# State-space matmuls with two lag halves in 32 weight columns, and six more sets of attention tiles on VectorE

## The chip, the cores and the metric

The kernel runs on one core of one Trainium2 chip. The metric is the device time of one execution in microseconds. Before the change the median of three runs is 829.91 us, with 829.02 us as the lowest and 830.75 us as the highest.

## The reference

The result mixes two branches of the same input `x` (2048 rows of 512 channels, bf16):

- `a`: softmax attention without a mask, 32 heads of 16 channels, `softmax(q k^T / 4) v`, then the product with `wo`. The scores are 32 x 2048 x 2048 numbers, and each needs an exponential.
- `b`: a long convolution for each channel. The kernel `K[d, l]` of 2048 lags is the real part of a sum over 128 complex states, `sum_n C[d,n] dB[d,n] exp(l dt A[d,n])`; `b = conv(x, K) + x * Dskip`, causal.
- The gate is `g = sigmoid(sum(x * gate_w))`, one number for each row, and the output is `g * a + (1 - g) * b`.

```python
    x = A_x
    g = _sigmoid((x * gate_w).sum(-1, keepdims=True))
    a = _A_ref(x, A_wqkv, A_wo)
    b = _B_ref(x, B_A_re, B_A_im, B_B_re, B_B_im, B_C_re, B_C_im, B_log_dt, B_Dskip)
    return g * a + (1 - g) * b
```

## The kernel before

**Attention.** The scores come in 2048 tiles of 128 keys by 512 queries, three tiles to a group, so 683 groups. For each group TensorE makes the scores in one of two PSUM buffers, `SC0` and `SC1` (`qk`), ScalarE takes the exponential of the group in one instruction (`ex`, line 907) into a ring of slots `ET` and, from group `NSG` on, also `EX`, and TensorE multiplies the result with the values into `OA` (`pv`). A score buffer is free again when all three of its tiles were read.

**Sets on VectorE.** Some tiles skip ScalarE. A set takes four tiles, each as the third tile of its own group, so such a group has only two tiles (1024 columns) for ScalarE. VectorE reads each of the four from PSUM with one `tensor_scalar` (`bits`, line 928), which makes the bit pattern of a bf16 power of two, and then finishes the four together (`batch`: two masks, line 939, and one product, line 947, on 2048 columns). The table `WIN` says in which groups sets may start, how many groups lie between two of them, and, as its last number, how much idle VectorE time a set must find. The kernel before has 71 sets.

**Convolution.** The channels go in 16 blocks of 32. For each block VectorE multiplies tables (`tables`, line 1197), TensorE makes the lags by matmuls with 32 weight columns of stride 128 (`kstage`, tiles `T` and `Z`), VectorE turns them round (`Kt`, `Ks`, lines 1233 to 1239), and they go to DRAM (`kd`) and back as Toeplitz pieces `H` (line 1295). `ystage` (line 1320) convolves: for each of 128 pieces there are 16 lag steps `m`, and in each four matmuls side by side in four column groups of the array, with 16 weight columns and 128 - 8m moving columns from `U`. VectorE multiplies the sum with 1 - g (line 1327, tile `Yst`), and it goes through DRAM (`yd`) to `Yl`.

**Gate and output.** `gate` computes g by 16 matmuls over `xT` (line 1356). `outs` multiplies the attention rows with `wo` in 16 row tiles `lt`, and VectorE makes `MB * g + Yl` (line 1418); the last four tiles get their last quarter at the very end (line 1605).

**What sets the order.** There is no order at run time: a planner on the host (`Sched`, `Prog`) keeps one clock for each engine and queue, from a cost `c` written at each operation, and writes each engine's instruction list. After each exponential it fills TensorE, VectorE and the DMA queue of SyncE with pieces of the other work, by their due times. It models the loading of TensorE's instructions in blocks of 256 (`BLOCK`, `pt`), and adds matmuls on zeros (`zero`, tile `wm`) so that the array's activity stays at a wanted level; `a` at each matmul is its share of that. All matmuls are recorded through one helper, so the profile shows all of them at line 661; they are told apart by tiles.

## Time and profile before

| What | Value |
|---|---|
| median of three runs | 829.91 us |
| the profiled execution | 830.66 us, span 828.7 us |
| ScalarE busy | 808.6 us (98%) |
| VectorE busy | 743.4 us (90%) |
| TensorE matmul busy | 686.8 us (83%), 15986 instructions |
| weight loads | 311.3 us (38%) |
| mean DMA rate | 112 GB/s |

The span is the time from the first to the last instruction in the trace, and the execution is some 2 us longer. Durations of neighbouring instructions on one engine overlap by some tens of nanoseconds, so a group's mean is more than the distance at which instructions follow each other; where that matters the count in a window of known length is used. In rows of groups the columns are: line, engine, operation, output<-input, shapes and count, then busy time and mean ns of one, then the idle time before them and what ended it. In rows of windows an engine's busy time is followed by the count of its instructions.

### The profile page before, as it was taken

The page shows a single profiled execution, that of the slowest core. Times are in us where ns is not written, and L with a number is a line of the kernel's source. Part 1 is how long each engine was busy: PE and PEld are TensorE (multiplying, and loading weights), DVE is VectorE, ACT ScalarE, POOL GpSimd, SP SyncE. Part 2 cuts the span into 40 slices and gives each one's busy share as a digit, 9 for nine tenths or more (in the row PEclk, how much of TensorE's full clock was granted, in tenths as well). Part 3 has the DMA queues.
Part 4 walks back from the last instruction along what each step waited for, and adds up shares of the span by engine and source line. Part 5 has one row for each costly group of instructions (what it writes and reads, how often), then busy time and mean ns, then how long its engine had stood idle before and what let it go on. Part 6 is the DMA issues. An engine that isn't in the chain of part 4 may idle for free.

```text
span 828.7 us, 35337 instructions
## 1 busy us (share of the span) xinstructions
PE 686.8 (83%) x15986; PEld 311.3 (38%) x16013; DVE 743.4 (90%) x1231; ACT 808.6 (98%) x692; POOL 10.2 (1%) x16
## 2 busy tenths in 40 slices
PE   7778787888788888898888988888887888878885
PEld 3232332333244444444454434444442444422221
DVE  7998998999999998899889889888998979699973
ACT  7999999999999999999999999999999999999995
POOL 4000000000000000000000000000000000000000
PEclk9999999999999999999999989999999999999998
DMA  9453001243566654654565555545566655410000
GB/s 194 99 109 52 7 8 17 52 132 112 165 161 172 151 138 125 171 150 121 133 139 129 151 135 131 137 121 142 128 166 118 184 148 149 104 24 21 23 32 26
DMA packets 182111, 92.75 MB, mean 112 GB/s; under 512 B 119237, under 2 KB 176966, under 8 KB 181578
## 3 DMA queue, kind: packets, MB, share of 16 engines
q1 hardware_dynamic: 180234, 89.58, 43.9%
q8 instruction: 126, 2.06, 1.1%
q10 hardware_dynamic: 1728, 0.92, 0.6%
q14 instruction: 23, 0.19, 0.1%
HBM read 64.47 MB, written 17.32 MB: 99 GB/s over the span
## 4 chain that ended last, share of the span: by engine, by line
ACT 91%; DVE 4%; PE 3%; DMA 1%; issue 0%; ACTq 0%; DVEq 0%
ACT ET L907 71%; ACT EX L907 19%; DVE DZ L928 2%; PE SC L661 1%; PE MB L661 1%; PE OA L661 1%; DVE DU L947 1%; DMA ldt<-in_B_log_dt_dram 1%; DVE fo L1418 0%; DVE DU L939 0%; DVE OT L963 0%; DVE DZ L939 0%; ACT L907 0%; ACT L1508 0%; ACTq L623 0%
## 5 line engine op out<-in xcount | busy, mean ns | idle before, releaser
L907 ACT ACTIVATE ET<-SC 128x1536 bf16<-128x1536 f32 (+1 forms) x530 | 648.9, 1538 | 3.4 <-PE SC L661 3.3
L661 PE MATMUL SC<-Qm,KT 32*128 32x512 bf16 x2048 | 277.6, 386 | 122.8 <-ACT ET L907 85.9
L928 DVE TENSOR_SCALAR DZ<-SC 128x512 uint16<-128x512 f32 x284 | 189.7, 685 | 35.2 <-PE SC L661 33.7
L907 ACT ACTIVATE EX<-SC 128x1024 bf16<-128x1024 f32 (+1 forms) x153 | 184.3, 1370 | 2.1 <-PE SC L661 1.9
L661 PEld LDWEIGHTS SC<-Qm,KT 32*128 32x128 bf16 x2048 | 70.6, 91 | 288.1 <-ACT ET L907 200.2
L661 PE MATMUL OA<-ET,VE 128*32 128x512 bf16 x1394 | 154.2, 392 | 1.4 <-ACT ET L907 0.9
L661 PE MATMUL OA<-wm 128*32 128x256 bf16 (+3 forms) x773 | 153.9, 354 | 1.2 <-DVE wm L714 1.2
L661 PEld LDWEIGHTS MB<-U,H 128*16 128x16 bf16 x8192 | 113.3, 108 | 46.1 <-issue 29.1
L661 PE MATMUL MB<-U,H 128*16 128x72 bf16 (+15 forms) x8192 | 128.1, 198 | 2.3 <-issue 2.2
L947 DVE TENSOR_TENSOR DU<-DZ,DU 128x2048 bf16<-128x2048 bf16 x71 | 87.3, 1233 | 0.8
L979 DVE TENSOR_TENSOR T<-B,DL 128x512 bf16<-128x512 bf16 x192 | 69.6, 418 | 0.0
L661 PEld LDWEIGHTS OA<-ET,VE 128*32 128x32 bf16 x1394 | 39.2, 93 | 77.3 <-issue 72.9
L661 PE MATMUL OA<-EX,VE 128*32 128x512 bf16 x370 | 55.6, 394 | 0.1
L661 PEld LDWEIGHTS MB<-T,Z 128*32 128x32 bf16 x2048 | 51.5, 178 | 9.1 <-issue 6.6
L661 PE MATMUL MB<-T,Z 128*32 128x64 bf16 (+1 forms) x2048 | 52.3, 246 | 0.0
L939 DVE TENSOR_SCALAR DU<-DZ 128x2048 uint16<-128x2048 uint16 x71 | 49.6, 705 | 0.7
L939 DVE TENSOR_SCALAR DZ<-DZ 128x2048 uint16<-128x2048 uint16 x71 | 49.6, 700 | 0.4
L661 PEld LDWEIGHTS OA<-wm 128*32 128x32 bf16 (+2 forms) x773 | 40.2, 95 | 13.9 <-issue 12.1
L979 DVE TENSOR_TENSOR ft<-FP,L 128x1024 f32<-128x1024 f32 (+1 forms) x32 | 34.8, 1123 | 0.4
L1327 DVE TENSOR_TENSOR Yst<-MB,gt 128x512 bf16<-128x512 f32 x32 | 21.9, 685 | 8.2 <-PE MB L661 8.2
L661 PE MATMUL OA<-DU,VE 128*32 128x512 bf16 x284 | 27.9, 383 | 0.3 <-DVE DZ L939 0.3
L661 PE MATMUL OA<-DZ,VE 128*32 128x512 bf16 x284 | 27.9, 381 | 0.0
(129 smaller groups left out, 461.4 us busy)
## 6 DMA issues: line engine op xcount, KB each, us to landing
H<-gm_kd SPq DMA_DIRECT2D x256, 128.0 KB, 3.4
U<-gm_xs SPq DMA_DIRECT2D x96, 136.0 KB, 2.9
U<-gm_xs SPq DMA_DIRECT2D x32, 134.2 KB, 3.0
T<-B SPq DMA_DIRECT2D x32, 128.0 KB, 2.6
gm_bd<-B16s SPq DMA_DIRECT2D x3, 1024.0 KB, 5.6
B<-gm_bd SPq DMA_DIRECT2D x12, 256.0 KB, 4.0
gm_kd<-Ks SPq DMA_DIRECT2D x64, 40.0 KB, 2.9
gm_xs<-xP SPq DMA_DIRECT2D x16, 136.0 KB, 4.8
```

The costliest lines, as they stand in the source:

```text
L661: op("PE", lambda t: t.matmul(out(), lhsT(), rhs(), start=start, stop=stop, skip_group_check=True, **kw), R, W, c=c, lat=.15, a=a, cfg=cfg)
L907: op("ACT", lambda a: a.activation(E(at, [[1, 512 * n]]), sc(0, [[1, 512 * n]]), AF.Exp, scale=DH ** -0.5), [(sc, i, g) for i in range(n)] ...
L928: op("DVE", lambda v: v.tensor_scalar(z.u16(512 * k, [[1, 512]]), sc(1024, [[1, 512]]), XS, XB, ALU.mult, ALU.add), [(sc, 2, g)], [(z, k, ...
L939: op("DVE", lambda v: v.tensor_scalar(t.u16(0, [[1, 2048]]), z.u16(0, [[1, 2048]]), a, o, ALU.bitwise_and, ALU.bitwise_or), R, W, c=.07 + ...
L947: op("DVE", lambda v, h=h, n=n: v.tensor_tensor(u(n * h, [[1, n]]), z(n * h, [[1, n]]), u(n * h, [[1, n]]), ALU.mult), R + [(u, 0, ("m", i ...
L979: op(eng, lambda v: v.tensor_tensor(o(), a(), b_(), f), R, W, c=c)
L1327: op("DVE", lambda v, w=w, h=h: v.tensor_tensor(Yst(1024 * w + 64 * h, [[128, R8], [4, 16], [1, 4]]), MB(0, [[1, R8], [R8, 16], [NC, 4]]), ...
```

## The change

- The lag steps of `ystage` go from 16 to 8. A weight tile now has 32 columns: for each of 16 phases one column for lag steps 0 to 7 and one for 8 to 15, on neighbouring PSUM partitions. The matmuls have 128 to 72 moving columns. The second half's result belongs 1024 rows later, so `Yst` and `yd` hold both halves, `Yl` gets the first and a new tile `Yl2` the second.
- `outs` adds both halves for row tiles 8 to 15 by two matmuls with the identity `idb` into the same PSUM sum; VectorE then only copies. So that the sum is right, the attention rows of these tiles get g earlier: one more product on the reciprocals `Rz` for query blocks 16 and up, with g in the layout `gq`.
- `gate` reads `xT` in contiguous rows of 512; its result goes out in pieces of four, `gt` is loaded for both halves by eight transfers and `gq` by five more.
- The table products go from twelve of 512 columns for a block to four of 1024 and four of 512. The lags' copy into `Ks` is four instructions in place of three.
- `H` is loaded by one transfer of 256 KB in place of two of 128 KB, with four buffers in place of five; `EX` is used from group 290 on in place of 214.
- The planner: a new model of TensorE's instruction loading, the batch of a set at a higher priority, and `WIN` asks for less idle time for each set. It comes to 77 sets.

```diff
-NSG = 214
+NSG = 290
...
-WIN = ((190,400,3,5,.9),(400,560,5,5,.9),(560,668,5,5,.6))
+WIN = ((190,400,3,5,.4),(400,560,5,5,.4),(560,674,5,5,.3))
...
+TM = (2, 1)
...
-NHB = 5
+NHB = 4
...
-HN = 2
+HN = 1
...
-FETCH = 3.4
-KEEP = 24
+PHASE = 191
+LEAD = 20
+F1 = 4.5
+F2 = 5.1
+KEEP = 8
+FORE = 12
...
-        if eng == "PE":
-            self.pt += [self.tm["PE"]] * 2
...
+        if eng == "PE" and len(self.pt) + 1 >= self.edge():
+            at = max(at, self.land())
...
+        w = self._record(eng, fn, deps, eng, i, R, W)
+        if eng == "PE":
+            b = self.edge()
+            self.pt += [at] * (2 + max(w - 1, 0))
+            if len(self.pt) > b:
+                self.av.append(max(self.pt[b - LEAD] + F1, self.av[-1] + F2))
...
+    def edge(self):
+        return (len(self.av) - 1) * BLOCK + PHASE
+
+    def land(self):
+        return self.av[-1]
...
-                    k = len(self.p.pt) - BLOCK + KEEP + 2 * len(t.seg)
-                    if k >= 0 and t.up > 0:
-                        e = max(e, self.p.pt[k] + FETCH - t.cost)
+                    k = self.p.edge() - len(self.p.pt) - 2 * sum(isinstance(a, tuple) for a in t.seg)
+                    if t.up > 0:
+                        e = max(e, self.p.land() - t.cost - max(k - KEEP, 0) / FORE)
...
+    sb("Yl2", 8 * D)
+    sb("gq", 32, FP32)
...
-            sch.add(batch(i), 1)
+            sch.add(batch(i), 0)
...
+        qc = b // 8
+        if qc >= 2:
+            op("DVE", lambda v: v.tensor_tensor(Rz(16 * w, [[16, n], [4, 4], [1, 4]]), Rz(16 * w, [[16, n], [4, 4], [1, 4]]),
+                                                B["gq"](4 * (qc - 2), [[0, n], [1, 4], [8, 4]]), ALU.mult),
+               [(Rz, x) for x in K] + [(B["gq"], j) for j in range(4)], [(Rz, x) for x in K], c=.12)
...
-                for m in range(3):
-                    Dm = B[("DL16", "DL64", "DL80")[m]]
-                    for k, (xr, yr) in enumerate(((0, 0), (1, 2), (1, 0), (0, 1))):
-                        yield ("DVE", H5)
...
+                DT = B["DT"]
+                for k, (xr, yr) in enumerate(((0, 0), (1, 2), (1, 0), (0, 1))):
+                    m = 0
+                    for w in TM:
+                        yield ("DVE", dv(512 * w, 2))
+                        tt("DVE", lambda k=k, m=m, w=w, Tm=Tm: Tm((k // 2 * 112 + (16, 64)[k % 2] + 16 * m) * CB, [[16 * CB, w], [2 * CB, 8], [1, 2 * CB]]),
...
-                    ch = 32 * (blk % 4) + 16 * (j // 2) + 2 * (j % 2) + 4 * (k % 4) + k // 4
+                    ch = 32 * (blk % 4) + 4 * (j // 2) + 2 * (j % 2) + 8 * (k % 4) + k // 4
...
-            op("DVE", lambda v, q=q: v.tensor_copy(Ks(5 * HW * q + HW, [[16, 4], [HW, 4], [1, 16]]), Kt(256 * q, [[64, 4], [16, 4], [1, 16]])),
+            op("DVE", lambda v, q=q: v.tensor_copy(Ks(5 * HW * q + HW, [[8, 4], [HW // 2, 8], [1, 8]]), Kt(256 * q, [[64, 4], [8, 8], [1, 8]])),
...
-        op("DVE", lambda v: v.tensor_copy(Ks(1, [[5 * HW, 2], [16, 4], [1, 15]]), Kt(48, [[256, 2], [64, 4], [1, 15]])),
-           [(Kt, 0, blk), (Ks, "z")], [(Ks, 1, blk)], c=.17)
+        for q in range(2):
+            op("DVE", lambda v, q=q: v.tensor_copy(Ks(q * HW // 2 + 1 - q, [[5 * HW, 2], [8, 4], [1, 7 + q]]), Kt(48 + 7 * q, [[256, 2], [64, 4], [1, 7 + q]])),
+               [(Kt, 0, blk), (Ks, "z")], [(Ks, (1, q), blk)], c=.13)
...
-    UN = 16 * UW - R8 + 1
-    UL = 16 * UW // UN4
+    Yst, yd, Yl, Yl2 = B["Yst"], B["yd"], B["Yl"], B["Yl2"]
+    UN = 4 * UW - R8 + 1
+    UP = 16 * UW // UN4
...
-                n = UL if i < UN4 - 1 else UN - UL * (UN4 - 1)
-                dma("SP", lambda e, v=v, U=U, i=i, n=n: e.dma_start(U(UL * i, [[1, n]]), xs.dram(v * 16 * UW + R8 - 1 + UL * i, [[D * UW, T], [-1, R8], [1, n]])),
+                dma("SP", lambda e, v=v, U=U, i=i: e.dma_start(U(UP * i, [[1, UN]]),
+                                                               xs.dram((v // 2 * 32 + v % 2 * 4) * UW + 2 * UP * i + R8 - 1, [[D * UW, T], [-1, R8], [1, UN]])),
...
-                for m in range(NM):
+                for m in range(NM // 2):
                     n = NC - R8 * m
-                    c = max(.0305, .0005 + n / 2400)
-                    if m in (0, 3, 7, 11):
-                        yield ("PE", sum(max(.0305, .0005 + (NC - R8 * x) / 2400) for x in range(m, m + (4 if m else 3))))
+                    c = n / 2400 + .0005
+                    if m % 4 == 0:
+                        yield ("PE", sum((NC - R8 * x) / 2400 for x in range(m, m + 4)))
                     for j in range(4):
-                        mm(lambda q=q, j=j, n=n: MB(NC * q + NC - n, [[1, n]], 32 * j, T),
-                           lambda j=j, m=m, H=H: H(j * NM + m, [[HW, T]]),
+                        mm(lambda q=q, j=j, n=n: MB(NC * q + NC - n, [[1, n]], 32 * j, 32),
+                           lambda j=j, m=m, H=H: H(j * NM // 2 + m, [[HW // 2, 2 * T]]),
                            lambda q=q, j=j, n=n, U=U: U((4 * j + q) * UW + 1, [[1, n]]),
-                           [(H, i, hu) for i in range(HN)] + [(U, i, u) for i in range(UN4)], ky, q + m == 0, m == NM - 1, pos=(0, 32 * j), c=c if j == 0 else 0,
-                           a=n // 8, cfg="C")
+                           [(H, i, hu) for i in range(HN)] + [(U, i, u) for i in range(UN4)], ky, q + m == 0, m == NM // 2 - 1, pos=(0, 32 * j), c=c if j == 0 else 0,
+                           a=n // 4, cfg="C")
...
-            op("DVE", lambda v, w=w, h=h: v.tensor_tensor(Yst(1024 * w + 64 * h, [[128, R8], [4, 16], [1, 4]]), MB(0, [[1, R8], [R8, 16], [NC, 4]]),
+            op("DVE", lambda v, w=w, h=h: v.tensor_tensor(Yst(1024 * w + 4 * h, [[128, R8], [8, 16], [1, 4]]), MB(0, [[1, R8], [R8, 16], [NC, 4]]),
...
-            dma("SP", lambda e, j=j: e.dma_start(yd.dram(512 * blk + 128 * j, [[8192, T], [T * 8192, R8], [1, 128]]),
-                                                 Yst(1024 * w, [[128, R8], [1, 128]], 32 * j, T)),
-                [(Yst, (w, h), blk) for h in range(2)], [(yd, (blk, j))], c=.6, lat=3.5, b=.15)
+            dma("SP", lambda e, j=j: e.dma_start(yd.dram(512 * blk + 128 * j, [[8192, 2 * T], [8192 * 2 * T, R8], [1, 128]]),
+                                                 Yst(1024 * w, [[128, R8], [1, 128]], 32 * j, 2 * T)),
...
-        for h in range(2):
...
-            dma("SP", lambda e, h=h: e.dma_start(Yl(512 * blk + 256 * h, [[64, 4], [1, 64]]), yd.dram(512 * blk + 64 * h, [[8192, P], [128, 4], [1, 64]])),
-                [(yd, (blk, j)) for j in range(4)], [(Yl, (blk, h))], c=.6, lat=3, b=.42, pace=True)
+            n = 128 >> k
+            dma("SP", lambda e, k=k, y=y, n=n: e.dma_start(y(4 * n * blk, [[n, 4], [1, n]]), yd.dram(512 * blk + 8192 * k, [[8192 * 2, P], [128, 4], [1, n]])),
+                [(yd, (blk, j)) for j in range(4)], [(y, blk)], c=.6, lat=3, b=.5, pace=True)
...
-                   lambda c=c, q4=q4: xT(q4 * S + 32 * c, [[1, 32], [P, 16]]),
+                   lambda c=c, q4=q4: xT(q4 * S + 512 * c, [[1, 512]]),
...
-        op("DVE", lambda v: v.tensor_copy(gl(0, [[1, 512]]), MB(0, [[1, 512]])), [(MB, 0, 'gate')], key("gl"), c=.62)
+        op("DVE", lambda v: v.tensor_copy(gl(0, [[4, P], [1, 4]]), MB(0, [[1, P], [P, 4]])), [(MB, 0, 'gate')], key("gl"), c=.62)
...
-            dma("SP", lambda e, j=j: e.dma_start(B["gt"](0, [[16, R8], [1, 16]], 32 * j, T), B["gd"].dram(0, [[16, T], [16 * T, R8], [1, 16]])),
+            dma("SP", lambda e, j=j: e.dma_start(alt("gt", [[16, R8], [1, 16]], 32 * j), B["gd"].dram(0, [[16, T], [16 * T, R8], [1, 16]])),
...
+            yield ("SP", .6)
+            dma("SP", lambda e, j=j: e.dma_start(alt("gt", [[16, R8], [1, 8]], 32 * j + 1), B["gd"].dram(8, [[16, T], [16 * T, R8], [1, 8]])),
+                [(B["gd"], 0)], [(B["gt"], 4 + j)], c=.6, lat=2.5)
...
+        yield ("SP", .6)
+        dma("SP", lambda e: e.dma_start(B["gg"].dram(0, [[16, P], [1, 16]]), g(0, [[1, 16]])), key("g"), [(B["gg"], 0)], c=.6, lat=2.5)
+        for j in range(4):
+            yield ("SP", .6)
+            dma("SP", lambda e, j=j: e.dma_start(B["gq"](0, [[8, 4], [1, 8]], 32 * j, 32), B["gg"].dram(8, [[16, 32], [512, 4], [1, 8]])),
+                [(B["gg"], 0)], [(B["gq"], j)], c=.6, lat=2.5)
+        sch.mark("gq")
...
+            if lt >= 8:
+                for y, at, W in ((Yl, 8 * lt, 128), (Yl2, 8 * (lt - 8), 64)):
+                    yield ("PE", MM)
+                    mm(lambda: MB(0, [[1, 512]]), lambda: idb(0, [[1, P]]), lambda y=y, at=at, W=W: y(at, [[W, D // 8], [1, 8]]),
+                       [(idb, 0)] + [(y, k) for k in range(NBLK)], [(MB, 0, ('o', lt))], False, y is Yl2)
...
-            op("DVE", lambda v, lt=lt, o=o, off=off: v.scalar_tensor_tensor(o(off, [[1, D]]), MB(0, [[1, D]]), B["g"](lt, [[1, 1]]),
-                                                                            Yl(4 * lt, [[64, D // 4], [1, 4]]), ALU.mult, ALU.add),
...
+            if lt < 8:
...
+            else:
+                op("DVE", lambda v, o=o, off=off: v.tensor_copy(o(off, [[1, D]]), MB(0, [[1, D]])), [(MB, 0, ('o', lt))], W, c=.62)
...
-        op("DVE", lambda v, lt=lt, b=b, off=off: v.scalar_tensor_tensor(fo((lt % 4) * D, [[1, D]]), b(off, [[1, D]]), B["g"](lt, [[1, 1]]),
-                                                                     fp((lt - 12) * D, [[1, D]]), ALU.mult, ALU.add),
...
+        op("DVE", lambda v, lt=lt, b=b, off=off: v.tensor_tensor(fo((lt % 4) * D, [[1, D]]), b(off, [[1, D]]), fp((lt - 12) * D, [[1, D]]), ALU.add),
```

More of the change, by code (lines that the diff above doesn't have):

```diff
@@ L131, in __init__ @@
         self.pt = []
+        self.av = [0.0]
         self.marg = {}
@@ L223, in _record @@
             b.st[sl] = [{stream: idx}, {}]
+        return len(waits)
     def op(self, eng, fn, R=(), W=(), c=.1, lat=.085, a=0, cfg=None):
@@ L516, in declare @@
         sb(n, 2 * D, FP32)
-    for n in ("L16", "L64", "L80"):
-        sb("D" + n, 6 * D)
+    sb("DT", 3 * 6 * D)
     for n in ("L32", "M8", "M9"):
@@ L545, in declare @@
     B["MB"] = Buf("MB", "ps", 512, FP32)
-    for n, free in (("kd", 8 * NBLK * HR * HW), ("xs", T * D * UW), ("yd", D * S), ("bd", 8 * P * 4096), ("qd", D * S), ("od", D * S)):
+    for n, free in (("kd", 8 * NBLK * HR * HW), ("xs", T * D * UW), ("yd", 2 * D * S), ("bd", 8 * P * 4096), ("qd", D * S), ("od", D * S)):
         B[n] = Buf(n, "dr", free, BF16)
         B[n].t = nc.dram_tensor("gm_" + n, [free // P, P], BF16)
-    for n in ("gd", "gld"):
+    for n in ("gd", "gg", "gld"):
         B[n] = Buf(n, "dr", P * 16, FP32)
@@ L1024, in short @@
         yield ("DVE", .33 * w * parts)
-        op("DVE", lambda v: v.tensor_copy(d(0, [[w, parts * D], o]), x(0, [[1, parts * D], i])), [(x, 0)], [(d, 0)], c=.07 + .28 * w * parts)
+        op("DVE", lambda v: v.tensor_copy(d(at, [[w, parts * D], o]), x(0, [[1, parts * D], i])), [(x, 0)], [(d, (ky, 0))], c=.07 + .28 * w * parts)
         if neg:
@@ L1245, in kstage @@
                                                  Ks(0, [[HW, 10], [1, HW]], 32 * h, 32)),
-                [(Ks, (0, 0), blk), (Ks, (0, 1), blk), (Ks, 1, blk), (Ks, "z")], [(kd, (blk, h))], c=.7, lat=3.5, b=.26)
+                [(Ks, (a, q), blk) for a in range(2) for q in range(2)] + [(Ks, "z")], [(kd, (blk, h))], c=.7, lat=3.5, b=.26)
         sch.mark(f"kd{blk}")
@@ L1369, in gate @@
         yield ("DVE", .4)
-        op("DVE", lambda v: v.memset(B["gt"](0, [[1, NC]]), 0.0), [], [(B["gt"], j) for j in range(4)], c=.2)
+        op("DVE", lambda v: v.memset(B["gt"](0, [[1, NC]]), 0.0), [], [(B["gt"], j) for j in range(8)], c=.2)
         op("DVE", lambda v: v.tensor_scalar(gp(0, [[1, 16]]), ge(0, [[1, 16]]), 1.0, None, ALU.add), key("ge"), key("gp"), c=.17)
@@ L1388, in out_mm @@
         mm(lambda: b(off, [[1, 512]]), lambda: OnX(pi * 512 + 128 * r, [[1, 128]]), lambda: Wo(pi * D, [[1, D]]),
-           [(OnX, pi // 2 if qc < SPILL else pi), (Wo, 0)], [(b, sl, ('o', lt))], pi == first, pi == (2 if lt >= 12 and first == 0 else 3))
+           [(OnX, pi // 2 if qc < SPILL else pi), (Wo, 0)], [(b, sl, ('o', lt))], pi == first, pi == 3 and (lt < 8 or first == 3))
     def out_dma(lt):
```

37 lines of the change are left out of this document (22 added, 15 removed).

## The prediction

> **What bounds the kernel now.** I read first the page's busy shares, the chain that ended last and the groups.
>
> ```profile
> span 828.7 us, 35337 instructions
> ...
> PE 686.8 (83%) x15986; PEld 311.3 (38%) x16013; DVE 743.4 (90%) x1231; ACT 808.6 (98%) x692; POOL 10.2 (1%) x16
> ...
> ACT 91%; DVE 4%; PE 3%; DMA 1%; issue 0%; ACTq 0%; DVEq 0%
> ...
> L907 ACT ACTIVATE ET<-SC 128x1536 bf16<-128x1536 f32 (+1 forms) x530 | 648.9, 1538 | 3.4 <-PE SC L661 3.3
> ...
> L928 DVE TENSOR_SCALAR DZ<-SC 128x512 uint16<-128x512 f32 x284 | 189.7, 685 | 35.2 <-PE SC L661 33.7
> L907 ACT ACTIVATE EX<-SC 128x1024 bf16<-128x1024 f32 (+1 forms) x153 | 184.3, 1370 | 2.1 <-PE SC L661 1.9
> ```
>
> ScalarE is the bound: 98% busy, 91% of the chain, 5.5 us idle before its 683 exponentials. 284 groups have their third tile on VectorE, and one is short because 2048 is no multiple of 3: 285 exponentials of two tiles, 398 of three. Their cost comes from the chain in order of time (start, length, what) and from a stretch almost without waits (498.32 to 740 us).
>
> ```profile
> 11.59 1.45 ACT ET L907
> ...
> 13.56 53.73 ACT ET L907 x40
> ...
> 818.44 0.93 ACTq L623
> ```
>
> ```profile
> L907 ACT ACTIVATE ET<-SC 128x1536 bf16<-128x1536 f32 x63 | 94.4, 1643 | 0.0
> L907 ACT ACTIVATE ET<-SC 128x1024 bf16<-128x1024 f32 x88 | 91.1, 1237 | 0.1
> L907 ACT ACTIVATE EX<-SC 128x1024 bf16<-128x1024 f32 x42 | 45.0, 1247 | 0.0
> L907 ACT ACTIVATE EX<-SC 128x1536 bf16<-128x1536 f32 x28 | 43.8, 1632 | 0.0
> ```
>
> Three tiles take 53.73/40 = 1.343 us. The stretch holds 91 of these and 130 of two tiles in 241.7 us, so two tiles take (241.7 - 91 x 1.343)/130 = 0.919 us. A tile moved off ScalarE is worth 0.424 us. The stream from 11.59 to 818.44 us is 806.9 us; 398 x 1.343 + 285 x 0.919 = 796.4 us of it is exponentials, and 10.4 us is lost. The windows show where:
>
> ```profile
> 230.00:810.00 580.00, 496.80 (x13624) 238.51 (x13633) 523.14 (x855) 576.19 (x517) 0.00 (x0) 0.99 0.49 124
> ...
> 440.00:450.00 10.00, 9.28 (x278) 5.66 (x282) 9.96 (x17) 10.00 (x10) 0.00 (x0) 1.00 0.46 131
> ...
> 465.00:470.00 5.00, 4.72 (x109) 2.56 (x109) 4.06 (x6) 5.00 (x5) 0.00 (x0) 0.70 0.36 96
> ...
> 490.00:500.00 10.00, 9.47 (x220) 3.81 (x206) 8.35 (x14) 8.71 (x9) 0.00 (x0) 0.66 0.52 141
> ...
> 744.00:781.00 37.00, 31.75 (x275) 9.22 (x276) 36.57 (x56) 35.51 (x35) 0.00 (x0) 1.00 0.09 26
> ```
>
> Columns are PE, PEld, DVE, ACT, POOL, granted clock, DMA share, GB/s. Around 465 to 500 us the clock falls to 0.66-0.70, matmuls fill the time and ScalarE waits; at 744 to 781 us VectorE is full (36.57 of 37) and ScalarE lacks 1.5 us. From 230 to 810 us VectorE has 580.0 - 523.1 = 56.9 us free.
>
> **The change part by part.**
>
> *Six more sets on ScalarE.* 24 tiles less: 24 x 0.424 = **-10.2 us**, on the chain. One exponential more or less at the stretch's edges moves the two-tile price by 0.01 us, so the ends are -9.9 and -10.4.
>
> *The gate.* Its 16 matmuls read `xT` with a stride. They are in front of the scores on TensorE's list:
>
> ```profile
> 67.66 3.60 PE L661 MATMUL MB<-xT,gwT 128*32 128x512 bf16 x16
> ...
> 71.63 4.14 ACT L907 ACTIVATE ET<-SC 128x1536 bf16<-128x1536 f32 x3 [1.66 <-PE SC L661]
> ...
> L661 PE MATMUL MB<-xT,Wk 128*128 128x512 bf16 x52 | 16.0, 383 | 1.1 <-issue 0.9
> ```
>
> Contiguous rows of the same width cost 16.0/52 = 0.31 us each; four groups of four side by side are then some 1.2 us and not 3.6. ScalarE's wait of 1.66 us needs more than 1.9 us of delay, so it goes: **-1.7 us** (between 0 and -1.7). Its nine further transfers on SyncE's queue, and its result in pieces of four, lie between the gate and the first use of `gt`:
>
> ```profile
> L1378 SPq DMA_DIRECT2D gt<-gm_gd x4: 334/426/775, 85.1 to 87.1; - x4
> ...
> L661 PE MATMUL MB<-U,H x8192: 168/197/307, 224.0 to 727.7; 128*16 128x128 bf16 x13, 128*16 128x48 bf16 x13, 128*16 128x96 bf16 x13, 128*16 128x16 bf16 x13
> ```
>
> From 87 to 224 us there is room for a chain many times as long; without that cover the convolution would begin later by what the pieces take.
>
> *VectorE.* Work added and saved, by these rows; the first three are chain pieces from a full stretch, where distances show:
>
> ```profile
> 761.35 0.60 DVE DZ L928
> 761.95 0.60 DVE DZ L939
> ...
> 769.27 1.13 DVE DU L947
> ```
>
> ```profile
> L947 DVE TENSOR_TENSOR DU<-DZ,DU 128x2048 bf16<-128x2048 bf16 x71 | 87.3, 1233 | 0.8
> L979 DVE TENSOR_TENSOR T<-B,DL 128x512 bf16<-128x512 bf16 x192 | 69.6, 418 | 0.0
> L939 DVE TENSOR_SCALAR DZ<-DZ 128x2048 uint16<-128x2048 uint16 x71 | 49.6, 700 | 0.4
> ...
> L979 DVE TENSOR_TENSOR ft<-Z,DM 128x1024 bf16<-128x1024 bf16 x32 | 20.7, 686 | 0.4
> ...
> L969 DVE RECIPROCAL Rz<-OT 128x32 f32<-128x32 f32 x15 | 5.2, 347 | 0.0
> ...
> L1239 DVE CAST Ks<-Kt 128x120 bf16<-128x120 f32 x16 | 3.5, 218 | 0.0
> ```
>
> A set is 4 x 0.60 + 2 x 0.60 + 1.13 = 4.73 us (by mean durations 5.37), six are +28.4 (to 32.2). Table products: 192 at 69.6/192 = 0.36 become 64 at 0.36 and 64 at 20.7/32 = 0.65: -4.8; should the extra dimension of the 1024-column form cost its speed, it could not be more than two of 512 each, so 0. `Ks`: 16 more at 0.22, +3.5. The g product on `Rz`: nine at up to 0.35, +1.5 to +3. The output copies are simpler than what they replace, under 0.5. Sum **+29 us of VectorE**, 26 to 38. All of it lies beside ScalarE if it fits: of 56.9 us free some 10 go with the shorter span, so 56.9 - 10.2 - 29 = 18 us of 570 remain, 3%. What is late when it does not fit is the third tile's read: the score buffer stays taken, `qk` of the next group but one waits, then ScalarE.
>
> *TensorE.* 8192 convolution matmuls become 4096.
>
> ```profile
> L661 PEld LDWEIGHTS MB<-U,H 128*16 128x16 bf16 x8192 | 113.3, 108 | 46.1 <-issue 29.1
> L661 PE MATMUL MB<-U,H 128*16 128x72 bf16 (+15 forms) x8192 | 128.1, 198 | 2.3 <-issue 2.2
> ...
> L661 PEld LDWEIGHTS MB<-T,Z 128*32 128x32 bf16 x2048 | 51.5, 178 | 9.1 <-issue 6.6
> L661 PE MATMUL MB<-T,Z 128*32 128x64 bf16 (+1 forms) x2048 | 52.3, 246 | 0.0
> ...
> L661 PE MATMUL MB<-Wo,OnR 128*128 128x512 bf16 x40 | 13.7, 386 | 0.2 <-issue 0.2
> ```
>
> Now 128.1/8192 = 15.6 ns each, so 4096 at that price are 64 us; the nearest matmuls with 32 strided weight columns (`T,Z`) take 52.3/2048 = 25.5 ns, so 105 us. I take the latter, like in width and stride: -23 us, ends -64 and 0 (twice the price of now). Two identity matmuls for eight row tiles add 16 x 13.7/40 = 5.5 us. So TensorE has some 17 us more room, worth nothing on the chain but where TensorE is full (465 to 500 us).
>
> The Trainium skill, "TensorE: Matmul & The Clock Gate", section "LDWEIGHTS (loading the stationary operand)", has a load cost its columns divided by 1.2 in ns: 13.3 for 16 columns, 26.7 for 32. The rows agree, 113.3/8192 = 13.8 and 51.5/2048 = 25.1. By that rule 4096 loads of 32 columns take 109 us, as long as now, and the room on TensorE is nearer to 4 us than to 23; the sum below stays.
>
> *Transfers.* `H` doubles in size and is fetched by half as many transfers, with one buffer less.
>
> ```profile
> H<-gm_kd SPq DMA_DIRECT2D x256, 128.0 KB, 3.4
> ...
> B<-gm_bd SPq DMA_DIRECT2D x12, 256.0 KB, 4.0
> ```
>
> A piece lasts about (727.7 - 224.0)/128 = 3.9 us, so three pieces ahead are 11.7 us against 4.0 to land: hidden; without cover TensorE's list stands with the scores behind it. `yd` doubles and `Yl2` comes new, at a DMA share of 0.49: hidden. SyncE's queue has 128 issues less for `H` and some 9 more for the gate. `EX` from group 290: ScalarE's idle time above ends with score matmuls (3.3 and 1.9 us), never with a slot that comes free, so nothing, at worst waits like those of the last window above.
>
> *The tail.* One more product stands between reciprocal and normalization of the last block: **+0.2 us** (0 to 0.35).
>
> **The sum.** 828.7 - 10.2 - 1.7 + 0.2 = 817.0 us of span, if the other 8.7 us of loss stay: less at the clock's low place, more where VectorE is full. The profiled execution lies 1.96 us over its span and 0.75 over the median of the runs: 829.91 - 11.7 = **818.2 us**.
>
> **The rivals.**
>
> *VectorE becomes the bound (slower).* The extra 29 us leave 3% free, and reads of third tiles queue behind products of 1.13 us. Price: in the full window ScalarE lost 1.5 of 37 us, 4%; over 570 us that is 23 us, less 1.5 lost already, 818.2 + 21.5 = 839.7 us. It decides from a loss of 11.7/570 = 2.1%. For it: that window. Against: 440 to 450 us, VectorE 9.96 of 10 full and ScalarE 10.00. Chance 0.14; with 0.03 for a loss that just eats the gain.
>
> *TensorE's stretch goes.* With 4096 matmuls fewer the place at 465 to 500 us is gone and the clock holds, so half of the 8.7 us comes back: under 814 us. In that place the chain has
>
> ```profile
> 487.57 0.80 issue
> ```
>
> where TensorE waits for nothing that the profile shows; half as many convolution instructions would shorten it if it is their supply. The Trainium skill, "Runtime: NRT & Kernel Launch", section "Instruction fetch mechanics", holds the fetch to be hidden; no run here shows what this piece is. Chance 0.13.
>
> *The clock falls more often.* The new plan has other matmuls and zeros; one or two more places like 465 to 500 us, 3 us each, give 822 to 828 us. Chance 0.07.
>
> *The sets do not come.* Whether 77 sets stand in the program is fixed when it is built; they can only come and not pay, which is the first rival.
>
> **How the numbers follow.** Forecast, ScalarE the bound with about the losses of now (814 to 822 us): 0.63. With 0.13 and 0.07 faster is 0.83; same, within 0.2% or 1.7 us (about what a measurement of this kernel can tell from no change), 0.03; slower 0.14. Range 811 to 829 us: its low end is the sum with seven of the 8.7 us gone, its high end a loss on VectorE that leaves a gain of 1 us; left out are some 0.17.
>
> **What would show it.** Right: 308 reads by VectorE, two-tile exponentials 309, ScalarE still near 98% with idle under 8 us, VectorE near 94-95%, gate matmuls near 1 us with no wait behind, `U,H` matmuls between 64 and 105 us. Wrong: long waits of ScalarE for score matmuls that themselves wait for `DZ`; TensorE waiting for `H`; windows with the clock under 0.8 in number.

## The result and the profile after

The changed kernel takes 879.12 us (median of 4 runs, 876.42 to 880.24), the kernel before 829.51 us (4 runs, 829.02 to 830.75). The ratio is 1.0591, with a 95% interval from 1.0564 to 1.0618. The forecast of 818.2 us was wrong in its sign. The profiled execution took 879.35 us.

The page of the changed kernel; in rows of groups the columns are busy time, mean ns of one, idle time before and what ended it. ScalarE's records overlap by more than the tens of nanoseconds named above: in the prediction's rows of three tiles their mean is 1643 ns and their distance 1343. So for ScalarE starts are compared below, and means only with each other.

```profile
span 877.4 us, 27009 instructions
...
PE 717.2 (82%) x11931; PEld 313.2 (36%) x11960; DVE 808.9 (92%) x1234; ACT 849.0 (97%) x692; POOL 10.2 (1%) x16
...
ACT 74%; PE 13%; DVE 8%; DMA 3%; issue 1%; ACTq 0%; SPq 0%; DVEq 0%
...
L949 DVE TENSOR_SCALAR DZ<-SC 128x512 uint16<-128x512 f32 x308 | 213.9, 716 | 28.1 <-PE SC L682 26.9
...
L682 PEld LDWEIGHTS MB<-U,H 128*32 128x32 bf16 x4096 | 81.9, 146 | 27.9 <-issue 19.2
L682 PE MATMUL MB<-U,H 128*32 128x128 bf16 (+7 forms) x4096 | 88.1, 231 | 4.1 <-DMA H<-gm_kd 2.8
L682 PEld LDWEIGHTS MB<-T,Z 128*32 128x32 bf16 x2048 | 73.5, 243 | 6.4 <-issue 5.8
L682 PE MATMUL MB<-T,Z 128*32 128x64 bf16 (+1 forms) x2048 | 71.6, 282 | 0.0
...
L1005 DVE TENSOR_TENSOR T<-B,DT 128x1024 bf16<-128x1024 bf16 (+1 forms) x128 | 65.0, 547 | 0.0
```

Two things stand out. ScalarE is 97% busy, nearly as before, although the kernel is 49 us slower and ScalarE has 24 tiles less: its instructions have become longer (849.0 us busy in place of 808.6). And the lag stage's matmuls (`T,Z`), which do the same work as before, went from 52.3 to 71.6 us and their weight loads from 51.5 to 73.5. The only edit to these matmuls is the order of the channels `ch`.

One lag stage shows what happens beside it. Groups of before in 140 to 147 us, where the first lag stage lies:

```profile
L907 ACT ACTIVATE ET<-SC 128x1536 bf16<-128x1536 f32 x7 | 10.5, 2212 | 0.0
L661 PEld LDWEIGHTS MB<-T,Z 128*32 128x32 bf16 x128 | 3.2, 178 | 0.4 <-issue 0.2
...
L979 DVE TENSOR_TENSOR ft<-FP,L 128x1024 f32<-128x1024 f32 x2 | 2.5, 1292 | 0.0
```

The same of the changed kernel in 138 to 145 us, where its first lag stage lies:

```profile
L928 ACT ACTIVATE ET<-SC 128x1536 bf16<-128x1536 f32 x4 | 9.3, 3570 | 0.0
L682 PEld LDWEIGHTS MB<-T,Z 128*32 128x32 bf16 x120 | 4.5, 244 | 0.5 <-issue 0.4
L1005 DVE TENSOR_TENSOR ft<-FP,L 128x1024 f32<-128x1024 f32 x2 | 4.1, 2080 | 0.0
```

In these 7 us four exponentials run, at least in part, in place of seven; ScalarE begins three in place of five, without waiting, and VectorE's product of 1.29 us takes 2.08. The granted clock was 0.76 in the second stretch and 1.00 in the first. That it is not the clock is seen in the kernel before with the new order alone (below), in 140 to 147 us at a clock of 1.00:

```profile
L907 ACT ACTIVATE ET<-SC 128x1536 bf16<-128x1536 f32 x5 | 10.7, 3337 | 0.0
L661 PEld LDWEIGHTS MB<-T,Z 128*32 128x32 bf16 x105 | 4.0, 241 | 0.2 <-issue 0.2
```

For all runs the span can be taken apart by the starts of the exponentials in the trace. Where no lag matmuls run and the clock is full, the median from one start to the next is 1.33 us behind an exponential of three tiles and 0.90 us behind one of two, the same in every run. The counts times these medians give the undisturbed stream; what each interval has over its median is put down to the clock when the granted clock is low in over 0.3 of it, else to the lag stage when its matmuls run beside it, and else to other causes. A fall is a change of the granted clock from full to half in its records, those behind the last exponential included. All in us:

| Kernel | sets | span | to the first | undisturbed | lag stage | low clock | other | behind the last start | falls of the clock |
|---|---|---|---|---|---|---|---|---|---|
| before | 71 | 828.7 | 11.6 | 786.5 | 6.1 | 2.6 | 11.3 | 10.5 | 3 |
| after | 77 | 877.4 | 10.7 | 775.9 | 46.2 | 17.5 | 16.0 | 11.1 | 18 |
| after, old order in the lag stage | 77 | 831.9 | 11.4 | 776.2 | 6.0 | 14.8 | 12.8 | 10.6 | 17 |
| before, new order in the lag stage | 71 | 873.4 | 10.9 | 786.6 | 47.1 | 10.6 | 7.8 | 10.4 | 10 |
| old order throughout | 79 | 833.2 | 11.2 | 772.4 | 6.6 | 5.8 | 20.4 | 16.8 | 10 |
| the same, 72 sets | 72 | 847.7 | 11.4 | 784.4 | 5.8 | 14.5 | 21.6 | 9.9 | 18 |
| the same, 71 sets, activity 1400 | 71 | 835.1 | 11.4 | 786.5 | 7.3 | 5.4 | 14.6 | 10.0 | 7 |
| before, activity 1150 | 71 | 841.1 | 11.3 | 786.5 | 8.5 | 10.8 | 13.7 | 10.3 | 10 |
| before, 76 sets and new gate | 76 | 867.5 | 11.6 | 777.6 | 6.9 | 2.5 | 7.5 | 61.5 | 4 |
| before, 74 sets, new gate and tables | 74 | 828.7 | 11.0 | 781.0 | 7.5 | 6.2 | 12.1 | 10.9 | 6 |

From before to after the sets bring -10.6, the lag stage +40.1, the clock +14.9, other places +4.7, the start and the end -0.3: +48.8 of the 48.7 us. Where lag matmuls and a low clock meet in one interval the split is a choice: put down to the lag stage first, it has +43.9 and the clock +11.8.

### The profile page after: what moved, and what is told of

Read it like the earlier page. It is cut to its first block, busy times and chain, and to the rows that moved or that the text cites. A ratio compares the mean times of both kernels' runs of the same rounds, so it can differ in the third digit from the quotient of the medians.

```text
span 877.4 us, 27009 instructions
## 1 busy us (share of the span) xinstructions
PE 717.2 (82%) x11931; PEld 313.2 (36%) x11960; DVE 808.9 (92%) x1234; ACT 849.0 (97%) x692; POOL 10.2 (1%) x16
## 4 chain that ended last, share of the span: by engine, by line
ACT 74%; PE 13%; DVE 8%; DMA 3%; issue 1%; ACTq 0%; SPq 0%; DVEq 0%
ACT ET L928 61%; ACT EX L928 13%; PE SC L682 5%; PE OA L682 4%; PE MB L682 3%; DVE DZ L949 3%; DMA H<-gm_kd 2%; DVE DU L968 1%; DVE DZ L960 1%; DVE ft L1005 1%; DMA Wk<-in_A_wqkv_dram 1%; DVE Yst L1357 1%; DVE OT L984 1%; DVE DU L960 1%; DVE FP L1005 0%
## 5 line engine op out<-in xcount | busy, mean ns | idle before, releaser
L928 ACT ACTIVATE ET<-SC 128x1536 bf16<-128x1536 f32 (+1 forms) x555 | 707.0, 1567 | 12.0 <-PE SC L682 8.1
L949 DVE TENSOR_SCALAR DZ<-SC 128x512 uint16<-128x512 f32 x308 | 213.9, 716 | 28.1 <-PE SC L682 26.9
L928 ACT ACTIVATE EX<-SC 128x1024 bf16<-128x1024 f32 (+1 forms) x128 | 157.4, 1383 | 2.3 <-PE SC L682 1.9
L682 PE MATMUL OA<-wm 32*128 32x512 bf16 (+3 forms) x756 | 156.3, 373 | 1.2 <-DVE wm L735 1.2
L682 PEld LDWEIGHTS MB<-U,H 128*32 128x32 bf16 x4096 | 81.9, 146 | 27.9 <-issue 19.2
L682 PE MATMUL MB<-U,H 128*32 128x128 bf16 (+7 forms) x4096 | 88.1, 231 | 4.1 <-DMA H<-gm_kd 2.8
L682 PEld LDWEIGHTS MB<-T,Z 128*32 128x32 bf16 x2048 | 73.5, 243 | 6.4 <-issue 5.8
L682 PE MATMUL MB<-T,Z 128*32 128x64 bf16 (+1 forms) x2048 | 71.6, 282 | 0.0
L682 PEld LDWEIGHTS OA<-ET,VE 128*32 128x32 bf16 x1436 | 40.1, 94 | 80.6 <-issue 74.4
L1005 DVE TENSOR_TENSOR T<-B,DT 128x1024 bf16<-128x1024 bf16 (+1 forms) x128 | 65.0, 547 | 0.0
L984 DVE STREAM_TRANSPOSE OT<-OA 128x512 f32<-128x512 f32 x32 | 24.1, 753 | 8.4 <-PE OA L682 8.0
```

The lines of the kernel that those rows point to most:

```text
L682: op("PE", lambda t: t.matmul(out(), lhsT(), rhs(), start=start, stop=stop, skip_group_check=True, **kw), R, W, c=c, lat=.15, a=a, cfg=cfg)
L928: op("ACT", lambda a: a.activation(E(at, [[1, 512 * n]]), sc(0, [[1, 512 * n]]), AF.Exp, scale=DH ** -0.5), [(sc, i, g) for i in range(n)] ...
L949: op("DVE", lambda v: v.tensor_scalar(z.u16(512 * k, [[1, 512]]), sc(1024, [[1, 512]]), XS, XB, ALU.mult, ALU.add), [(sc, 2, g)], [(z, k, ...
L984: op("DVE", lambda v: v.transpose(OT(512 * w, [[1, 512]]), OA(0, [[1, 512]])), [(OA, 0, b)], [(OT, w, b)], c=.64)
L1005: op(eng, lambda v: v.tensor_tensor(o(), a(), b_(), f), R, W, c=c)
```

## The experiments

Theory A: the new channel order of the lag stage makes its reads disturb ScalarE and VectorE. Theory B, the prediction's slower rival: VectorE, with six sets more, is the bound. Theory C: the granted clock falls more often.

### The channel order, taken out and put in alone

The changed kernel with the old order in the lag stage alone:

```diff
-ch = 32 * (blk % 4) + 4 * (j // 2) + 2 * (j % 2) + 8 * (k % 4) + k // 4
+ch = 32 * (blk % 4) + 16 * (j // 2) + 2 * (j % 2) + 4 * (k % 4) + k // 4
...
-Dr(32 * blk + 4 * (j // 2) + 2 * (j % 2), [[8, 4], [1, 2]])
+Dr(32 * blk + 16 * (j // 2) + 2 * (j % 2), [[4, 4], [1, 2]])
```

> The changed kernel with one edit: the lag stage's matmuls (tiles T and Z) take their channels in the order of before, so the four column groups read 0, 2, 16 and 18 elements apart in place of 0, 2, 4 and 6. Everything behind is left, so the convolution gets the channels of a block in another order: the time is that of the same work. Theory A (this order makes the lag stage's matmuls slow and holds up VectorE, and the clock falls follow): mean of these matmuls back from 282 to about 246 ns, no VectorE read of a third tile over 1 us, clock 0.98 or more, 815 to 835 us. Theory B (VectorE has too much with six more sets) and theory C (the planner's new placement lets the clock fall): all of this stays, 870 to 880 us.

It took 833.97 us, one run, against 831.35 of before on the same chip (7 runs, 828.8 to 832.24): 45 us less than the changed kernel. In its page the lag stage's loads take 178 ns again, and VectorE's busy time is 43 us less than in the changed kernel:

```profile
PE 689.3 (83%) x11931; PEld 290.2 (35%) x11960; DVE 766.0 (92%) x1234; ACT 803.3 (97%) x692; POOL 10.2 (1%) x16
...
L682 PEld LDWEIGHTS MB<-T,Z 128*32 128x32 bf16 x2048 | 50.7, 178 | 8.3 <-issue 6.0
```

The clock did not come back: its mean is 0.954, expected were 0.98 or more, and there are 17 falls. So the channel order explains the 45 us and not most of the falls; those are left to Theory C.

The other way, the kernel before with only these two lines changed to the new order:

> The kernel before with the opposite edit: only the lag stage's channel order of the changed kernel (channels of the convolution in another order, same work). Theory A: these matmuls go from 246 to about 282 ns, some VectorE instructions take 1 to 2 us during the lag stage, the clock falls more often than its two times, 845 to 875 us. Theories B and C: within 3 us of the kernel before, 827 to 833 us.

It took 875.38 us (one run), 44 us more. The chain of waits in 225 to 300 us, in order of time (start, length, what), first of before and then of this run; the two programs have the same instructions and groups:

```profile
224.75 74.23 ACT ET L907 x61
```

```profile
223.88 76.26 ACT ET L907 x52
```

ScalarE never waits in either, and three lag stages lie in each. It does 52 exponentials in 76.26 us in place of 61 in 74.23. Part of this is the mix, since the slower run is at earlier groups: 7 of the 52 have two tiles, and 20 of the 61. By the medians the 52 are worth 66.2 us and the 61 72.7, so 10.1 us are lost in place of 1.6. Theory A holds both ways for the time; in this plan the new order also brings ten falls in place of three.

### Which operand it is

In the kernel before, the new order for the weights alone, and then for the moving side alone:

```diff
+c2 = 32 * (blk % 4) + 4 * (j // 2) + 2 * (j % 2) + 8 * (k % 4) + k // 4
...
-lambda ch=ch, t=t: Z(t // 2 * 4096 + ch, [[128, 32]])
+lambda ch=c2, t=t: Z(t // 2 * 4096 + ch, [[128, 32]])
```

> The kernel before, where only the weights of the lag matmuls (tile `Z`) are read at the new channels and the moving side (`T`) at the old ones; the lags mix two channels, so the numbers that leave it are not the convolution, the work is the same. If the weights' columns, two elements apart in the four column groups instead of 2 and 16, are what collides: weight loads of `T,Z` near 241 ns, two-tile and three-tile exponentials near 1.35 and 2.1 us beside them, 870 to 880 us. If it is the moving side: loads stay at 178 ns and the time at 828 to 835 us. If it needs both: something between, 840 to 860 us.

```diff
-lambda ch=ch, at=at, n=n: Tm(at + 2 * (ch % 32), [[2 * CB, n // 2], [1, 2]])
+lambda ch=c2, at=at, n=n: Tm(at + 2 * (ch % 32), [[2 * CB, n // 2], [1, 2]])
```

> The mirror image: the kernel before, where only the moving side (`T`) is read at the new channels and the weights (`Z`) at the old ones; again the lags mix channels and the work is the same. If the weights collide: 828 to 835 us and 178 ns a load. If the moving side does (four column groups 8 bytes apart in one row): matmuls of `T,Z` near 280 ns, the time at 870 to 880 us. If it needs both: 840 to 860 us.

Weights alone: 887.02 us, above its range. Moving side alone: 828.99 us (one run each; before 830.93, 7 runs). The loads, first by weights alone, then by the moving side alone:

```profile
L661 PEld LDWEIGHTS MB<-T,Z 128*32 128x32 bf16 x2048 | 83.0, 268 | 8.1 <-issue 7.7
```

```profile
L661 PEld LDWEIGHTS MB<-T,Z 128*32 128x32 bf16 x2048 | 51.3, 177 | 8.9 <-issue 6.4
```

It is the weights. The four loads side by side read columns of stride 128 from `Z`; in the old order they begin at elements 0, 2, 16 and 18, in the new one at 0, 2, 4 and 6, all four within 14 bytes of a row. The same index also changes the step from one `k` to the next, from 4 elements to 8; no run has the two apart, so that the distance between the four is what counts is not shown. Nor is it explained why the weights alone cost 12 us more than weights and moving side together (loads of 268 and 241 ns).

### VectorE's load

The changed kernel with the set table of before (72 sets):

```diff
-WIN = ((190,400,3,5,.4),(400,560,5,5,.4),(560,674,5,5,.3))
+WIN = ((190,400,3,5,.9),(400,560,5,5,.9),(560,668,5,5,.6))
```

> The changed kernel with the set table of before (each set must find 0.9, 0.9, 0.6 us of idle VectorE time; starts up to group 668), so fewer sets. Theory B: VectorE falls to about 90% and the time to 835 us or less. Theory A: a few sets less cost ScalarE 1.7 us each and change nothing of the lag stage: 865 to 890 us. Theory C: 865 to 890 us as well.

It took 891.45 us (one run), with VectorE busy 777.5 us (87%): less work on VectorE, and 12 us slower. With the run of 833.97 us, which keeps all 77 sets, Theory B falls as the cause of the 49 us.

The version with the old order also in `U`, `Yst`, `yd`, `Yl` and `Yl2` (79 sets, `EX` from group 306):

```diff
-xs.dram((v // 2 * 32 + v % 2 * 4) * UW + 2 * UP * i + R8 - 1, [[D * UW, T], [-1, R8], [1, UN]])
+xs.dram(v * 16 * UW + UP * i + R8 - 1, [[D * UW, T], [-1, R8], [1, UN]])
...
-Yst(1024 * w + 4 * h, [[128, R8], [8, 16], [1, 4]])
+Yst(1024 * w + 64 * h, [[128, R8], [4, 16], [1, 4]])
```

> The changed kernel with the channel order of before all the way: lag stage, U, Yst, yd, Yl and Yl2 (Yl and Yl2 are read in pieces of 4 and not 8 elements, loaded by 64 transfers and not 32; EX from group 306 because of its space). It computes the reference. Theory A: as the first run, 812 to 832 us, so faster than or equal to the kernel before. Theories B and C: 865 to 880 us.

It took 842.67 us (835.07 to 847.0, 4 runs), ratio 1.016 (1.0124 to 1.0195), so Theory A's range was missed. Without the lag stage's loss the plan is still slower than before. The four mean clocks were 0.974, 0.964, 0.959 and 0.957 at 835.07, 842.2, 843.14 and 847.0 us: the slower the execution, the lower its clock. The traced one, in the table above, is the fastest.

### The clock

The falls can be seen in the windows of the changed kernel with the old order in the lag stage (columns as in the prediction):

```profile
680.00:683.00 3.00, 2.08 (x26) 0.60 (x22) 3.00 (x5) 3.00 (x4) 0.00 (x0) 1.00 0.69 170
683.00:686.40 3.40, 2.39 (x32) 0.64 (x32) 3.15 (x6) 3.40 (x4) 0.00 (x0) 1.00 0.28 60
686.40:689.80 3.40, 3.39 (x29) 0.64 (x26) 3.23 (x5) 3.40 (x4) 0.00 (x0) 0.51 0.79 174
```

TensorE has work for 2.39 of 3.40 us, and in the next 3.4 us the clock is 0.51 and matmuls fill the time. The row before is no fuller, 2.08 of 3.00 us, and no fall stands right behind it, so this share alone does not decide.

The kernel before with fewer matmuls on zeros:

```diff
-FILL = 1300
-FILL2 = 1300
+FILL = 1150
+FILL2 = 1150
```

> The kernel before with fewer matmuls on zeros, wanted activity 1150 in place of 1300: the other way. If low activity lowers the clock and the clock costs time: mean clock from 0.99 to 0.95 to 0.97, 835 to 850 us. If the clock's falls in the changed kernel come from something else (bursts of convolution matmuls, instruction supply): clock 0.98 to 0.99 and 829 to 832 us.

842.06 us (840.91 and 843.21), ratio 1.0129 (1.0089 to 1.017), ten falls in place of three and 0.962 as mean clock. So the clock's price is shown on the old kernel: less activity, 11 us, of which 8 us more lie at a low clock. In the old order throughout, zeros were then added, sets taken away by the table of before, and both done together:

```diff
-FILL = 1300
-FILL2 = 1300
+FILL = 1500
+FILL2 = 1500
```

> The changed kernel with the old channel order throughout (as in the run of 842.67 us) and more matmuls on zeros: the planner's wanted activity goes from 1300 to 1500. If the rest of the loss is the clock, which falls where the array does little in a few microseconds: the granted clock goes from 0.96 to 0.97 back to 0.98 or more, the falls from some ten to under four, and the time to 818 to 828 us. If it is VectorE's fuller list: the clock may rise, and the time stays at 835 to 845 us.

```diff
-WIN = ((190,400,3,5,.4),(400,560,5,5,.4),(560,674,5,5,.3))
+WIN = ((190,400,3,5,.9),(400,560,5,5,.9),(560,668,5,5,.6))
```

> The changed kernel with the old channel order throughout and the set table of before (about 72 sets in place of 79, some 28 reads and 33 us of VectorE less). If VectorE's full list is what leaves TensorE without work, lowers the clock and so costs the rest: falls of the clock before which VectorE is full go from some seven to under three, the mean clock to 0.98 or more, and the time, with one set more than before and the gate's 1.7 us, to 822 to 829 us. If the falls come from the convolution in bursts of 32-column matmuls (much activity, then little), whatever VectorE does: clock 0.96 to 0.97 still, and 838 to 846 us.

> Between the two: the set table of before and wanted activity 1400 (1053 matmuls on zeros). By the first theory 821 to 829 us and a clock of 0.98; if zeros cost more than they give, between the other two runs.

> The same with the set table of before and wanted activity 1500 as well (1459 matmuls on zeros in place of 932). If low activity between bursts is the cause and VectorE's list made the fuller plan of 850 us slow: both causes are gone, clock 0.985 or more, 821 to 829 us. If the zeros themselves cost, by TensorE's time: 838 to 850 us at a high clock.

With 79 sets and 1500: 850.61 us (4 runs), no fewer falls (10). With 72 sets and 1300: 853.54 us (4 runs), ratio 1.0279 (1.0236 to 1.0322). With 71 sets and 1400: 840.07 us (2 runs), and 1500: 840.78 us (2 runs), with 7 and 5 falls. None came near the 818 to 829 us of the first theories. The mean clock of the 72 sets, and of 71 sets with 1400:

```profile
core 0: 847.7 us, clock 0.951
```

```profile
core 0: 835.1 us, clock 0.985
```

Zeros give back 13 us where VectorE has room. Fewer sets did not give fewer falls (18), and the clock was lower in each of four executions (0.939 to 0.951, against 0.957 to 0.974 with 79 sets), so a full VectorE does not by itself explain the falls. With 79 sets and 1500, nine of the ten falls stand behind stretches of 3.4 us where VectorE is busy for 98% or more. But so are 0.62 of the stretches at full clock that no fall follows; that Theory B's mechanism brings falls in this plan is possible and not shown.

More zeros in the kernel before (`FILL` and `FILL2` at 1450), and, in the old order throughout, half the activity counted for each 32-column matmul:

> The kernel before with wanted activity 1450 in place of 1300, so 1452 matmuls on zeros in place of 849, in the old plan with 16-column convolution. If TensorE has the room there and the clock at 465 to 500 us cost before some 4 to 6 us: 822 to 828 us at a clock of 0.99 or more. If zeros take time that TensorE needs: 832 to 850 us, with score matmuls late while the clock is at 1.

```diff
-a=n // 4, cfg="C")
+a=n // 8, cfg="C")
```

> The changed kernel with the old channel order throughout, where the planner counts each 32-column matmul of the convolution with half its activity, as much as a 16-column one of before (1036 matmuls on zeros in place of 901). If zeros left out beside the convolution are the cause: clock 0.98, under five falls, 822 to 834 us. If the falls come where no convolution runs: clock 0.95 to 0.97 and 835 to 847 us as with full credit.

They took 847.9 us (4 runs, ratio 1.0196, 1.0163 to 1.023) and 876.88 us (2 runs). Neither brought what its first theory said, and the loss is not in the number of falls: four falls in the first, nine in the second. In the second 63 us lie behind the start of the last exponential and in the first 27.

### The parts alone, and what a set costs

The kernel before with 76 sets alone, then with the contiguous gate as well (second hunk, and `gl` and `gld` to fit), and before with the planner's new model alone:

```diff
-WIN = ((190,400,3,5,.9),(400,560,5,5,.9),(560,668,5,5,.6))
+WIN = ((190,400,3,5,.8),(400,560,5,5,.4),(560,674,5,5,.3))
...
-xT(q4 * S + 32 * c, [[1, 32], [P, 16]])
+xT(q4 * S + 512 * c, [[1, 512]])
```

> The kernel before with 76 sets in place of 71 (another set table) and nothing else: old convolution, old channel order, old model. If the sets do what the prediction said and the clock's falls come from the new convolution or the new model: 20 tiles x 0.424 = 8.5 us less, 821 to 824 us, at most four falls, clock 0.985 or more. If the fuller VectorE brings the falls: clock 0.95 to 0.97, 830 to 843 us.

> The same with the gate of the changed kernel that reads `xT` in contiguous rows (old layout of its result otherwise). The wait of 1.66 us behind the gate's matmuls goes: 1.7 us less than the run without it, 819 to 823 us by the first theory. A new plan can move the clock's falls either way by some 3 us each.

```diff
-FETCH = 3.4
-KEEP = 24
+PHASE = 191
+LEAD = 20
+F1 = 4.5
+F2 = 5.1
+KEEP = 8
+FORE = 12
...
+        if eng == "PE" and len(self.pt) + 1 >= self.edge():
+            at = max(at, self.land())
```

> The kernel before with the new model of TensorE's instruction loading in the planner and nothing else. If the model is what places work and zeros badly: clock 0.95 to 0.975, eight or more falls, 835 to 848 us. If it is not: 826 to 833 us at a clock of 0.985 or more.

874.6 us (ratio 1.0514, 1.0495 to 1.0534), 869.05 us (1.044, 1.0425 to 1.0456) and 853.06 us (1.0249, 1.022 to 1.0278). All three lie above every range that was expected. But six, four and four falls only: neither the sets nor the gate nor the model bring the 17 or 18, nor do the table products (six falls in the last run below). What is left is the new convolution with its transfers, the batch's priority, and the parts together; no run had any of these alone, so that it is the new convolution is likely and not shown. It comes in bursts: of the stretches of 3.4 us from the first to the last convolution matmul, 25 of 148 hold none of them in the trace of before, and 74 of 150 in the old order throughout.

The time went elsewhere. With 76 sets and the gate, the stream of exponentials ends 12 us earlier than before, and then comes this (windows behind the stream):

```profile
807.00:820.00 13.00, 3.58 (x150) 2.21 (x140) 1.44 (x2) 0.21 (x1) 0.00 (x0) 0.74 0.15 29
820.00:860.00 40.00, 25.63 (x57) 5.57 (x56) 12.48 (x18) 0.00 (x0) 0.00 (x0) 0.50 0.11 37
```

and the chain there, in order of time:

```profile
813.26 1.87 DMA gm_yd<-Yst
815.62 2.19 DMA Yl<-gm_yd
818.10 0.76 DVE fo L1418
818.91 1.90 PE MB L661 x4
820.84 0.76 DVE fo L1418
821.65 1.90 PE MB L661 x4
```

The last convolution is finished only behind the last exponential, and all 16 row tiles of the output follow one by one at half the clock. VectorE makes the tables for the convolution; that the additional sets push them back is likely, but with the new model alone (72 sets) the convolution is late too. The last convolution matmul stands behind group 602 of 683 in the program before, 586 after, 682 with 76 sets or half credit, 657 with the new model and 642 with the zeros at 1450; the time behind the last start is 10.5, 11.1, 61 to 63, 35 and 27 us.

### 74 sets with the last convolution early

The kernel before with the gate and the 1024-column table products of the change, `EX` from group 290, and two set tables of 74 sets with which the last convolution stays early (groups 599 and 597):

```diff
-WIN = ((190,400,3,5,.9),(400,560,5,5,.9),(560,668,5,5,.6))
+WIN = ((190,400,3,5,.9),(400,560,5,5,.8),(560,610,5,5,.6),(610,676,4,5,.2))
...
+WIN = ((190,400,3,5,.9),(400,560,5,5,.75),(560,610,5,5,.6),(610,676,3,5,.1))
```

> The kernel before with the contiguous gate, the 1024-column table products of the change, and a set table chosen so that the last convolution stays where it was (after group 599 of 683; before 602, in the run with 76 sets 682): 74 sets, `EX` from group 290. Convolution, channel order and model are those of before. If the sets pay 0.424 us a tile as long as the convolution is early: 12 x 0.424 = 5.1 us and 1.7 us of the gate, 823 us (820 to 826), behind the last exponential some 9 to 10 us. If VectorE's load as such costs more than a set brings: 830 to 840 us.

> The same with the sets of the last window as near as three groups to each other and a slightly lower bound in the middle one; also 74 sets, last convolution after group 597. Nearly the same plan: 820 to 826 us by the first theory, and the distance between the two runs says what the order alone is worth; more than 4 us apart would mean that such plans scatter by more than the gain.

The first took 836.04 us (6 runs), ratio 1.0055 (1.0034 to 1.0077), the second 828.92 us (10 runs), ratio 0.9978 (0.9962 to 0.9995) to 830.85 of before on this chip: 0.2% faster than the kernel before, which is as little as the prediction held for measurable. Neither came near 823 us. In the second the undisturbed stream is 5.5 us shorter, and lag stage, clock and other places take 5.8 us more. The two tables differ in little and are 7 us apart: the stalls that a plan happens to have can be worth more than the three sets that were added (5.1 us).

## Why the prediction was wrong

- **The step that failed** is the change "part by part": its list of parts passes over the lag stage's new channel order, `ch` and the index of `Dr`, and so costs it at nothing. It is worth +40.1 us of the 48.7 in the taken-apart span (+43.9 by the other split), and 44 and 45 us in the runs that put it in and took it out. The prediction priced the layout of the convolution's and the gate's operands, and not that of an operand in a stage whose work stayed the same.
- **Six more sets, -10.2 us:** -10.6 us in the undisturbed stream, by 308 reads, and -10.3 with the old order. Right on the chain; what a set can cost when the plan makes the convolution late was not seen, and in this plan (group 586) it did not arise.
- **Gate, -1.7 us:** right. The 16 matmuls take 1.0 us in place of 3.6 and the wait behind them is gone. With and without it the sets' runs are 5.5 us apart; a fall of the clock right behind the old gate's wait makes it more than 1.7.
- **VectorE, +29 us (26 to 38):** +22.6 us with the old order (766.0 - 743.4), a little under the range: `Ks` cost 1.2 us and not 3.5. The table products gave -4.6 for -4.8. In the changed kernel it is +65.5, so the channel order adds 43 to VectorE's busy time.
- **TensorE, -23 us (ends -64 and 0) and +5.5:** the convolution's matmuls went from 128.1 to 88.1 us, -40, and the identity products took 5.3 us. Inside the ends; the row I went by (`T,Z`, 25.5 ns) was too dear, they cost 21.5 ns. The rule of the Trainium skill, "TensorE: Matmul & The Clock Gate", section "LDWEIGHTS (loading the stationary operand)", would have the new loads at 109 us; they took 81.9, 20.0 ns each, so here the trace does not agree.
- **Transfers hidden:** nearly. TensorE waited 2.8 us before convolution matmuls for `H`.
- **The tail, +0.2 us:** +0.6 us.
- **The other 8.7 us of loss stay:** they did not. The rival "the clock falls more often" was right in kind and wrong in size: it had one or two more places of 3 us and a chance of 0.07; there were 15 more falls, and +14.9 us, and with the old order in the lag stage, where no gain is left (833.97 us), the low clock alone takes +12.2, more than the sets bring. What made the falls stays open. Other places have +4.7 us. The rival with VectorE as the bound had the right sign by a wrong mechanism.

The signs named for a failure, long waits for score matmuls and windows under 0.8, were there in part; the main one, longer exponentials with no wait at all, was not on the list.

## What to carry to other kernels

Cost every index that a change touches, in stages too whose work stays the same: the columns that weight loads read can slow other engines that wait for nothing, and a busy share of 97% does not show it; compare the mean time of the same instruction in the same stage. A planner's engine with some room free is also the maker of what a later stage needs, so ask when the last piece of that stage comes, not only whether the sum fits. And before a plan is changed, look at how thin TensorE's list gets in a few microseconds, since nearly all falls here stood behind thin stretches.

## What was not expected of the hardware

- Weight loads of four column groups that begin at elements 0, 2, 4 and 6, with a stride of 128 from column to column, took 243 ns, and 178 ns at 0, 2, 16 and 18. Beside the former exponentials and f32 products on VectorE, whose tiles all lie in SBUF, took longer (2.08 in place of 1.29 us for one product), while score matmuls did not (385 ns before, 384 with the new order alone, in 140 to 147 us). The Trainium skill, "SBUF — State Buffer", section "Who interferes with whom", says that TensorE and ScalarE never wait on anyone there and that only the pair of ports shared by VectorE and GpSimd causes contention. The run with the weights' index alone does not agree: one index of TensorE's reads took ScalarE's busy time from 808.6 to 864.8 us, with GpSimd at 10.2 us in both. Which path they meet in, and which distance or step of the columns is enough, was not tried and stays open.
- The granted clock fell behind stretches of 3.4 us in which TensorE mostly had work for 0.5 to 0.8 of the time (16 of 17 in the changed kernel with the old order in the lag stage). The Trainium skill, "TensorE: Matmul & The Clock Gate", section "What's actually happening", has it halve after an idle window of that length; here a thin one was enough, as the rows above show. Why others are not followed by a fall is open: in that run 0.40 of the stretches at full clock without a fall behind them had no more work than 0.8 either.
